# First loads of step B on other queues, with later stores and moved idle matmuls, in a fused FFT mixing and MoE kernel

## The chip, the cores and the metric

The kernel runs on one core of a Trainium2 chip. The metric is the device time of one execution in microseconds (us). Engines are named as in the profile: PE is TensorE (matmuls), PEld its weight loads, DVE is VectorE, ACT is ScalarE, POOL is GpSimd, SP is SyncE. SP, ACT and POOL each have a queue from which they issue DMA transfers; a transfer issued from such a queue waits in that engine's program order until what it reads is ready.

## The reference, cut to what matters

```python
X = np.fft.rfft(x, axis=1)                       # x: 4 x 3008 x 256
Xr, Xi = X.real, X.imag
Yr = Xr @ w_r - Xi @ w_i + b_r
Yi = Xr @ w_i + Xi @ w_r + b_i
Yr = sign(Yr) * maximum(abs(Yr) - 0.01, 0)
Yi = sign(Yi) * maximum(abs(Yi) - 0.01, 0)
y = np.fft.irfft(Yr + 1j * Yi, n=3008, axis=1)
x = y.reshape(12032, 256)
h = x @ w_in                                     # 256 x 2048, float64 weights
g = maximum(h, 0) + alpha * minimum(h, 0)
out = (g @ w_out).astype(float32)                # 2048 x 256
```

## The kernel before, in words

The sequence of 3008 is split as 47 x 64. For each of the four batches the transform and its inverse run in four steps, each a set of matmuls against a table.

Step A transforms along the 47 in 16 groups: `a_load` (L341) brings rows of x by SP, `a_mm` (L382) multiplies two matmuls a group into one of the three banks of `ps_f`, `a_evac` (L396) copies the bank to SBUF. For batch 0 the result stays in SBUF, in `a0_s`, and ScalarE and VectorE take turns at the copies. For the other batches ScalarE copies into a tile `ast`, and its store to DRAM is appended to a list, which `put` (L334) later issues from SP.

Step B transforms along the 64, in 12 pairs: `b_load` (L412) loads a pair in two halves of 128 KB into one of three buffers `bt`, for batch 0 out of `a0_s` by POOL, else by SP; `b_mm` (L423) multiplies with the table `rb_s`, `b_evac` (L432) takes the high part by ScalarE, `b_evac2` (L450) the low part by VectorE, and POOL then writes negated copies of a part of both (L457). The mix with w_r and w_i is `m_mm` (L465): a bias product (L471), then 24 matmuls (L478), in which the six with w_r come ahead of the six with w_i, twice; the ones with w_i read the negated copies. w_r and w_i are loaded raw (`load_mix`) and split into a high part by ScalarE and a low part by POOL (`split_mix`, L226). `m_evac` (L499) clips: ScalarE writes a tile `Yc` (L504), VectorE the output Y (L505). Step C (`c_mm`, `c_evac`, L545, L563) transforms back along the 64 and stores to DRAM from ScalarE's queue; step D transforms back along the 47 and feeds the two MoE layers, which fill the rest of the time from about 105 us on.

Beside all this the float64 weights of the MoE layers are converted into pairs of float32 parts. `conv_load` (L254) loads 512 KB of raw weights by SP into one of three slots; the conversion is a list of operations (`conv_first`, L265; `conv_second`, L280), of which `pump(n)` (L312) runs the next n, four for each raw weight once it is under way: the absolute value by ScalarE and a step of the weight before by VectorE (L275, L290), a clamp by VectorE (L276), two ScalarE, one VectorE and one POOL operation (L284 to L287), then VectorE and POOL operations (L293, L294, L277). A slot is free for the next load once L290 and L285 have read it.

The order of the work is written by hand. Batch 0's 16 groups of step A are followed by the first EARLY = 4 groups of batch 1 (L1006 to L1016). When the group n = NG is reached, batch 0's last group has just been evacuated. After that a loop over t (L1036) runs for each pair: the product of step B for pair t, the loads of pair t + 3, evacuations of the pairs before, the mix for pair t - 1, step C for pair t - 3, then PT[t] operations of the conversion, and some loads. `keep_warm(n)` (L985) issues n matmuls on a small tile of zeros that nobody reads. The last entry before the loop is `keep_warm(WARM)`.

The early groups' outputs use buffers that step B and C need later: the tags of `A1_TAGS` (L981) are, for the four groups, two of the buffers that step C copies into, then `Yt`, then `Yc`, which `m_evac` writes first for pair 0 in the loop's round 2.

Of the kernel before, what the change touches and what calls it, by code (L numbers as in the profile page):

```python
# [93 lines left out]
def fft_mix_moe(ctx, tc, x, w_r, w_i, b_r, b_i, w_in, w_out, alpha, la, rb, lc, rd, lf, cf, sel, out):  # L94
    nc = tc.nc
# [40 lines left out]
    def split(src, hi, lo, e_hi, e_lo):  # L136

        if e_hi is A:
            A.activation(out=hi, in_=src, func=AF.Copy)
        else:  # L140
            e_hi.tensor_copy(out=hi, in_=src)
        e_lo.tensor_tensor(out=lo, in0=src, in1=f(hi), op=ALU.subtract)
# [24 lines left out]
    def half(h):  # L167
        t = const.tile([128, 2, FH * 2 * C], F32R, tag=f"half{h}", name=f"w{h}")
        wi_h[h] = t[:, 0].rearrange("p (w k f) -> p w k f", w=2, k=CT)
        wo_h[h] = t[:, 1].rearrange("p (m w f) -> p m w f", w=2, f=C)  # L170

    def load_tables():
        nc.sync.dma_start(out=rd_s, in_=rd)
        nc.sync.dma_start(out=alpha_s, in_=alpha.rearrange("(k p) -> p k", p=128))
# [33 lines left out]
    def load_mix(*tags):  # L208
        for w, tag in zip((w_r, w_i), tags):
            t = work.tile([128, CT, C], F32, tag=tag, name="wm_f", bufs=1 if tag[1] in "tc" else None)  # L210
            nc.sync.dma_start(out=t, in_=w.rearrange("(k p) f -> p k f", p=128))
            mix_w.append(t)

    def load_rb(n0, n1):
        nc.sync.dma_start(out=rb_s[:, n0:n1], in_=rb[:, n0:n1])

    def load_cf(n0, n1):
        nc.gpsimd.dma_start(out=cf_s[:, n0:n1], in_=cf[:, n0:n1])
# [7 lines left out]
    def split_mix():  # L226
        for t, w in zip(mix_w, mix):
            split(t, w[:, 0], w[:, 1], A, G)
        mix_w.clear()
# [24 lines left out]
    def conv_load():  # L254

        m, i = divmod(conv_m[0], 2)
        conv_m[0] += 1
        k = conv_m[0] % 3
        raw = cw_s[:, NSLOT + 8 * k:NSLOT + 8 * k + 8].rearrange("p (k n) f -> p k (n f)", k=2)
        raw = raw.rearrange("p k (n w) -> p k n w", w=2)  # L260
        src = w_out.bitcast(U32)[256 * m:256 * m + 256] if i else w_in.bitcast(U32)[:, 512 * m:512 * m + 512]
        nc.sync.dma_start(out=raw.rearrange("p k n w -> p k (n w)"), in_=src.rearrange("(k p) f -> p k f", p=128))
        conv_raw.append((raw, m, i))
# [70 lines left out]
    def put(*queues):  # L334
        for n, (o, i) in enumerate(stores):
            (queues or (nc.sync,))[n % max(len(queues), 1)].dma_start(out=o, in_=i)
        stores.clear()
# [44 lines left out]
    def a_mm(b, g):  # L382
        ps = ps_f.tile([NQ, 2, C], F32, tag="f", name="ps_a")
        pa[b, g] = ps
        if b < 2:
            ts = x_rows(b, g)
            n = 2 // len(ts)
            for i, t in enumerate(ts):
                PE.matmul(ps[:, n * i:n * i + n], lf_s, t, start=True, stop=True)
            return  # L390
        hi, lo = xp.pop((b, g))
        PE.matmul(ps, la_s[:, 0], hi, start=True, stop=False)
        PE.matmul(ps, la_s[:, 1], hi, start=False, stop=False)
        PE.matmul(ps, la_s[:, 0], lo, start=False, stop=True)

    def a_evac(b, g):  # L396
        ps = pa.pop((b, g))
        if b == 0:
            st = a0_s[:, g]
        else:  # L400
            tag = A1_TAGS[g] if b == 1 and g < len(A1_TAGS) else "zst"
            st = work.tile([NQ, 2, C], F32, tag=tag, name="ast", bufs={"bt": 3, "zst": 3, "Yt": 1, "Yc": 1}.get(tag))
        if b == 0 and g % 2:
            V.tensor_copy(out=st, in_=ps)
        else:
            A.activation(out=st, in_=ps, func=AF.Copy)
        if b:
            stores.append((ad[b][:, 2 * g:2 * g + 2], st))

    bt, xs, xe, yc, ys = {}, {}, {}, {}, {}  # L410

    def b_load(b, q):  # L412
        t = work.tile([128, 2, C], F32, tag="bt", name="bt", bufs=3)
        if b == 0:
            src = a0_s.rearrange("(w s q) g r c -> q w s (g r) c", w=4, s=2)[q]
        else:
            src = ad[b].rearrange("(w s q) r c -> q w s r c", w=4, s=2)[q]

        for k in range(2):
            (nc.gpsimd if b == 0 else nc.sync).dma_start(out=t[:, k], in_=src[:, k])  # L420
        bt[b, q] = t

    def b_mm(b, q):  # L423
# [551 lines left out]
    EARLY = 4  # L975
    FILL = 14
    C0 = 2
    PT = [1, 2, 3, 3, 3, 3, 3, 3, 3, 3, 4, 4]
    TAIL = [['me', 1], ['ce', 3], ['cm', 2], ['cm', 1], ['ce', 2], ['ce', 1], ['d'], ['f', 4], ['e'], ['f', 6]]
    WARM = 70  # L980
    A1_TAGS = ("zst", "zst", "Yt", "Yc", "bt", "bt", "bt", "Xh", "Xl", "Xh", "Xl", "zst", "zst", "Yc")  # L981
    X1_TAGS = {4: ("Yl", "Yl"), 5: ("os", "Yt"), 6: ("gh",) * 4}
    idle = const.tile([128, 128], BF16, name="idle")
# [1 line left out]
    def keep_warm(n):  # L985
        ps = ps_f.tile([128, 512], F32, tag="f", name="ps_idle")
        for _ in range(n):
            PE.matmul(ps[:, 0:128], idle, idle, start=True, stop=True)

    with tc.manual_schedule():  # L990
# [8 lines left out]
        for g in range(EARLY // 2):  # L999
            a_load(1, g)  # L1000
        load_mix("Yh", "Yh")
        load_rb(4, 12)
        conv_tags.update(v1=("yh", "yl"), ex=("xh", "xh"), lf=("xl", "xl"))
        for _ in range(C0):
            conv_load()
        seq = [(0, g) for g in range(NG)] + [(1, g) for g in range(EARLY)]  # L1006

        for n, (b, g) in enumerate(seq):
            a_mm(b, g)
            if n >= 1:  # L1010
                a_evac(*seq[n - 1])
            if n == NG:
                for q in range(3):
                    b_load(0, q)
                split_mix()
                bias_parts()  # L1016
        a_evac(*seq[-1])
        half(0)
        put()
        load_tables()  # L1020
        keep_warm(WARM)

        def run(fn, q, *args):
            if 0 <= q < NPAIR:
                fn(0, q, *args)
# [8 lines left out]
                a1[0] = g + 1  # L1034

        for t in range(NPAIR + 1):  # L1036
            run(b_mm, t)
            run(b_load, t + 3)
            run(c_evac, t - 4)
            run(b_evac, t)  # L1040
            run(m_evac, t - 2)
            run(m_mm, t - 1, ps_h)
            run(b_evac2, t)
            run(c_mm, t - 3)
            if t < NPAIR:
                pump(PT[min(t, len(PT) - 1)])
            if t in (2, 5):
                load_rb(2 * t + 8, 2 * t + 14)
            if t < 8 and t % 2 == 0:
                load_cf(3 * t, 3 * t + 6)  # L1050
            if 5 <= t < 10:
                a_load(1, t - 3)
            if t == 10:
                half(1)
                conv_m[1] = FT
# [144 lines left out]
        for k in range(len(spairs) + SLAG):  # L1200
# [9 lines left out]
            if k >= SLAG:  # L1210
                n, t = spairs[k - SLAG]
# [43 lines left out]
```

## Time and profile before

| what | value |
|---|---|
| median of 3 runs | 1350.1 us (1348.96 to 1350.62) |
| the profiled execution's own time | 1350.56 us |
| its span in the profile | 1348.8 us |
| PE busy | 1335.5 us, 99% of the span |
| DVE, ACT, POOL busy | 77%, 56%, 28% |
| chain that ended last | PE 89%, DVE 3%, DMA 3% |

A row of a timeline gives the start and the duration in us, the engine, the source line, the operation, out<-in, the count, and in brackets how long the engine was idle before it and what ended that. Rows of SPq are DMA issues on SP's queue. A matmul's end is modelled, so rows of PE overlap by a little. Landing is the time from a DMA's issue to the semaphore that says that it is complete.

### The profile page before, as it was taken

What the parts mean: (1) busy time and instruction counts of PE and PEld (TensorE: products, weight loads), DVE (VectorE), ACT (ScalarE), POOL (GpSimd) and SP (SyncE); (2) the same over time, 40 slices, a digit from 0 to 9 for tenths busy, and PEclk for the clock granted to TensorE, in tenths of its full rate; (3) what the DMA queues carried; (4) which work ended last, traced back from release to release, by engine and by line L of the source; (5) the groups of instructions that cost most, each with busy time, mean ns of one, the idle gap of its engine ahead of it and who ended that gap; (6) DMA issues with size and microseconds to landing.
All of it is one profiled execution on the core that took longest, in us unless ns stands there. A gap on an engine that the chain in (4) does not pass through costs nothing.

```text
span 1348.8 us, 25138 instructions
## 1 busy us (share of the span) xinstructions
PE 1335.5 (99%) x9200; PEld 1250.7 (93%) x9200; DVE 1034.9 (77%) x1938; ACT 761.0 (56%) x1526; POOL 375.5 (28%) x400
## 2 busy tenths in 40 slices
PE   8999999999999999999999999999999999999998
PEld 4979999999999999999999999999999999999998
DVE  2767856776777777776768888888888888888885
ACT  3566655665566645555555555655555555555653
POOL 3864642222321222222221211121112111211222
PEclk9999999999999999999999999999999999999999
DMA  9974223342333312111110110111011101110001
GB/s 236 251 202 140 81 94 106 105 138 74 98 115 112 111 54 79 53 51 47 36 36 2 40 28 4 37 28 28 6 35 28 28 6 35 29 28 8 22 17 29
DMA packets 88119, 89.67 MB, mean 66 GB/s; under 512 B 42317, under 2 KB 70448, under 8 KB 87995
## 3 DMA queue, kind: packets, MB, share of 16 engines
q1 hardware_dynamic: 79700, 77.02, 20.1%
q0 software_dynamic: 5168, 8.02, 2.2%
q10 hardware_dynamic: 3127, 3.01, 0.7%
q8 instruction: 73, 1.20, 0.4%
q14 instruction: 51, 0.42, 0.1%
HBM read 50.49 MB, written 34.34 MB: 63 GB/s over the span
## 4 chain that ended last, share of the span: by engine, by line
PE 89%; DVE 3%; DMA 3%; issue 2%; ACT 1%; SPq 1%; POOL 0%; ACTq 0%; DVEq 0%; POOLq 0%
PE ps_h L794 24%; PE ps_h L689 13%; PE ps_m L491 6%; PE ps_o L895 6%; PE ps_o L896 6%; PE ps_o L894 6%; PE ps_d L620 4%; PE ps_o L728 3%; PE ps_o L727 3%; PE ps_o L726 3%; PE ps_b L428 2%; PE o_last L727 1%; PE o_last L728 1%; PE o_last L726 1%; PE o_last L894 1%
## 5 line engine op out<-in xcount | busy, mean ns | idle before, releaser
L794 PE MATMUL ps_h<-yh,w 128*128 128x512 f32 (+1 forms) x960 | 315.6, 389 | 0.0
L833 POOL TENSOR_TENSOR l<-t,h 128x512 fp32r<-128x512 f32 x98 | 127.0, 1296 | 496.5 <-ACT h L831 456.9
L794 PEld LDWEIGHTS ps_h<-yh,w 128*128 128x128 f32 x960 | 180.0, 188 | 33.2
L798 DVE SCALAR_TENSOR_TENSOR sq<-sq,beta_s,ps_h 128x512 f32<-128x512 f32 (+1 forms) x240 | 167.9, 732 | 54.5 <-ACT sq L797 53.6
L689 PE MATMUL ps_h<-yh,w 128*128 128x384 f32 (+1 forms) x704 | 207.0, 337 | 1.3 <-DVE q L696 1.3
L794 PE MATMUL ps_h<-yl,w 128*128 128x512 f32 (+1 forms) x480 | 186.2, 388 | 0.0
L696 DVE SCALAR_TENSOR_TENSOR q<-q,beta_s,ps_h 128x384 f32<-128x384 f32 (+1 forms) x192 | 115.1, 600 | 91.8 <-ACT q L695 90.9
L700 ACT ACTIVATE gh<-q 128x384 fp32r<-128x384 f32 (+1 forms) x192 | 99.1, 516 | 148.0 <-DVE q L696 145.3
L701 POOL TENSOR_TENSOR gl<-q,gh 128x384 fp32r<-128x384 f32 (+1 forms) x90 | 96.8, 1075 | 274.9 <-ACT gh L700 265.4
L813 ACT ACTIVATE dh<-sq 128x768 fp32r<-128x768 f32 x112 | 94.8, 846 | 117.8 <-DVE sq L798 75.8
L797 ACT ACTIVATE sq<-ps_h 128x512 f32<-128x512 f32 (+1 forms) x240 | 133.2, 586 | 26.9 <-PE ps_h L794 25.6
L689 PEld LDWEIGHTS ps_h<-yh,w 128*128 128x128 f32 x704 | 129.3, 189 | 4.4 <-DVE q L696 1.3
L695 ACT ACTIVATE q<-ps_h 128x384 f32<-128x384 f32 (+1 forms) x192 | 91.9, 479 | 62.1 <-PE ps_h L689 61.4
L831 ACT ACTIVATE h<-t 128x512 fp32r<-128x512 f32 x98 | 62.0, 633 | 105.2 <-DVE t L829 103.0
L689 PE MATMUL ps_h<-yl,w 128*128 128x384 f32 (+1 forms) x352 | 116.5, 331 | 0.0
L728 PE MATMUL ps_o<-w,gl 128*128 128x256 f32 x384 | 108.0, 281 | 0.6 <-POOL gl L701 0.6
L727 PE MATMUL ps_o<-w,gh 128*128 128x256 f32 x384 | 107.8, 281 | 0.0
L726 PE MATMUL ps_o<-w,gh 128*128 128x256 f32 x384 | 107.7, 280 | 0.0
L794 PEld LDWEIGHTS ps_h<-yl,w 128*128 128x128 f32 x480 | 90.5, 189 | 13.6
L828 DVE TENSOR_TENSOR dl<-sq,dh 128x768 fp32r<-128x768 f32 x98 | 93.4, 953 | 3.9 <-ACT dh L813 3.9
L896 PE MATMUL ps_o<-l,sw_a 128*128 128x256 f32 x294 | 82.0, 279 | 0.0
L894 PE MATMUL ps_o<-h,sw_a 128*128 128x256 f32 x294 | 81.9, 279 | 0.0
(214 smaller groups left out, 3618.5 us busy)
## 6 DMA issues: line engine op xcount, KB each, us to landing
zt<-zd SPq DMA_DIRECT2D x32, 384.0 KB
zd<-zst SPq DMA_DIRECT2D x37, 256.0 KB
ad<-ast SPq DMA_DIRECT2D x48, 192.0 KB
bt<-ad SPq DMA_DIRECT2D x72, 128.0 KB
xt<-in_x SPq DMA_DIRECT2D x21, 320.0 KB
out<-oT SPq DMA_DIRECT2D x152, 32.0 KB
cw_s<-in_moe_w_in SPq DMA_DIRECT2D x8, 512.0 KB
cw_s<-in_moe_w_out SPq DMA_DIRECT2D x8, 512.0 KB
```

Source lines behind the costliest of these rows:

```text
L689: PE.matmul(ps, wi_h[m // FH][:, w, ct, 128 * (m % FH):128 * (m % FH) + 128], a[:, ct, 0:n], start=(k == 0), stop=(k == 3 * CT - 1))
L696: V.scalar_tensor_tensor(out=q, in0=q, scalar=beta_s[:, m:m + 1], in1=ps, op0=ALU.mult, op1=ALU.add)
L700: A.activation(out=hi, in_=q, func=AF.Copy)
L726: PE.matmul(a, hi[:, t], w[:, 0], start=(i, k) in first, stop=False)
L727: PE.matmul(a, hi[:, t], w[:, 1], start=False, stop=False)
L728: PE.matmul(a, lo[:, t], w[:, 0], start=False, stop=(i, k) in last)
L794: PE.matmul(ps, wi_h[m // FH][:, w, ct, 128 * (m % FH):128 * (m % FH) + 128], a[:, ct, 0:w1], start=(k == 0), stop=(k == 3 * CT - 1))
L797: A.activation(out=q[:, j], in_=ps, func=AF.Relu, scale=-1.0)
L798: V.scalar_tensor_tensor(out=q[:, j], in0=q[:, j], scalar=beta_s[:, m:m + 1], in1=ps, op0=ALU.mult, op1=ALU.add)
L833: G.tensor_tensor(out=l24, in0=t24, in1=f(h24), op=ALU.subtract)
L894: PE.matmul(o, wh, gh, start=first, stop=False)
L896: PE.matmul(o, wh, gl, start=False, stop=last)
```

## The change

The loads of pairs 0 and 1 of step B are issued half by SP and half by ScalarE, and come ahead of the table part `load_rb(4, 12)` and the two first raw weights in SP's program; pair 2 stays with POOL. The split of the mixing weights goes behind the last evacuation of step A. The early groups' four stores (`put`) go from ahead of the loop to its round 1, and the two small tables of `load_tables` (the table of step D and alpha) to its round 6. The 70 idle matmuls ahead of the loop become 16, and 12 are issued at the head of round 1. PT has one operation fewer in rounds 0 and 1 and one more in rounds 8 and 9; the sum stays at 35.

```diff
-    def b_load(b, q):
+    def b_load(b, q, queues=None):
+        queues = queues or ((nc.sync,) * 2 if b else (nc.gpsimd,) * 2)
...
-            (nc.gpsimd if b == 0 else nc.sync).dma_start(out=t[:, k], in_=src[:, k])
+            queues[k].dma_start(out=t[:, k], in_=src[:, k])
...
-    PT = [1, 2, 3, 3, 3, 3, 3, 3, 3, 3, 4, 4]
+    PT = [0, 1, 3, 3, 3, 3, 3, 3, 4, 4, 4, 4]
...
-    WARM = 70
+    WARM = 16
...
         load_mix("Yh", "Yh")
-        load_rb(4, 12)
         conv_tags.update(v1=("yh", "yl"), ex=("xh", "xh"), lf=("xl", "xl"))
-        for _ in range(C0):
-            conv_load()
...
             if n == NG:
-                for q in range(3):
-                    b_load(0, q)
-                split_mix()
+                both = nc.sync, nc.scalar
+                b_load(0, 0, both)
+                b_load(0, 1, both)
+                load_rb(4, 12)
+                b_load(0, 2)
+                for _ in range(C0):
+                    conv_load()
                 bias_parts()
         a_evac(*seq[-1])
+        split_mix()
         half(0)
-        put()
-        load_tables()
         keep_warm(WARM)
...
         for t in range(NPAIR + 1):
+            if t == 1:
+                keep_warm(12)
             run(b_mm, t)
...
+            if t == 1:
+                put()
+            if t == 6:
+                load_tables()
             if 5 <= t < 10:
                 a_load(1, t - 3)
```

## Rows read from the trace of the kernel before

**Rows 1.** The page's busy times: engine, busy us, share of the span, instructions.

```profile
PE 1335.5 (99%) x9200; PEld 1250.7 (93%) x9200; DVE 1034.9 (77%) x1938; ACT 761.0 (56%) x1526; POOL 375.5 (28%) x400
```

**Rows 2.** Timeline of PE, from the start to pair 4 of step B.

```profile
1.00 4.02 PE L988 MATMUL ps_idle<-idle 128*128 128x128 bf16 x36 [1.00 <-DVE idle L991]
...
20.69 2.79 PE L389 MATMUL ps_a<-xt,lf_s 94*96 94x512 f32 x6 [0.78 <-DVE lam_s L199]
...
25.52 4.07 PE L988 MATMUL ps_idle<-idle 128*128 128x128 bf16 x70
30.42 1.80 PE L428 MATMUL ps_b<-rb_s,bt 128*128 128x128 f32 x12 [0.83 <-issue]
33.10 0.71 PE L428 MATMUL ps_b<-rb_s,bt 128*128 128x128 f32 x4 [0.87 <-DMA bt<-a]
...
34.59 0.40 PE L478 MATMUL ps_m<-wi_s,Xh 128*128 128x256 f32 x2
...
36.72 1.05 PE L428 MATMUL ps_b<-rb_s,bt 128*128 128x128 f32 x8
...
40.67 1.05 PE L428 MATMUL ps_b<-rb_s,bt 128*128 128x128 f32 x8
...
45.50 1.05 PE L428 MATMUL ps_b<-rb_s,bt 128*128 128x128 f32 x8
```

**Rows 3.** Timeline of POOL, 17 to 34 us.

```profile
21.29 4.11 POOL L420 DMA_DIRECT2D bt<-a  x6 [16.19 <-DVE bias_h L201]
25.51 1.28 POOL L142 TENSOR_TENSOR wr_s<-wm_f,wr_s 128x512 fp32r<-128x512 f32 x1
...
31.85 1.37 POOL L420 DMA_DIRECT2D bt<-a  x2 [3.85 <-PE ps_b L428]
33.25 0.41 POOL L457 TENSOR_SCALAR Xh<-Xh 128x256 fp32r<-128x256 f32 x1
```

**Rows 4.** Landing of step B's loads by POOL: the first half, then all 24 halves.

```profile
L420 POOL DMA_DIRECT2D bt<-a x1: 735/735/735, 21.3 to 21.3; - x1
DMA to landing us min/median/max: 9.0/9.0/9.0
...
L420 POOL DMA_DIRECT2D bt<-a x24: 679/690/807, 21.3 to 68.5; - x24
...
DMA to landing us min/median/max: 4.2/7.8/9.9
```

**Rows 5.** Windows: stretch, length, then PE, PEld, DVE, ACT, POOL busy, clock, DMA share, GB/s.

```profile
24.50:30.40 5.90, 5.01 (x72) 4.25 (x73) 0.00 (x0) 1.59 (x4) 3.40 (x4) 1.00 1.08 244
...
70.00:75.00 5.00, 5.00 (x41) 4.85 (x40) 4.86 (x7) 2.64 (x6) 4.37 (x4) 1.00 1.07 265
```

**Rows 6.** Timeline of ScalarE, 17 to 125 us.

```profile
22.70 0.63 ACT L139 ACTIVATE wr_s<-wm_f 128x512 fp32r<-128x512 f32 x1 [3.02 <-DMA wm_f<-in_w_r]
...
23.95 1.54 ACT L406 ACTIVATE ast<-ps_a 96x512 f32<-96x512 f32 x3
...
80.49 0.63 ACT L284 ACTIVATE w<-conv 128x512 fp32r<-128x512 f32 x1 [1.43 <-DVE conv L290]
```

**Rows 7.** Timeline of SP's DMA issues, 17 to 140 us.

```profile
24.55 4.61 SPq L336 DMA_DIRECT2D ad<-ast  x4
...
30.37 1.55 SPq L174 DMA_DIRECT2D alpha_s<-in_moe_alpha  x1
31.96 2.55 SPq L262 DMA_DIRECT2D cw_s<-in_moe_w_in  x1
...
62.10 4.58 SPq L360 DMA_DIRECT2D xt<-in_x  x4
...
70.24 9.29 SPq L360 DMA_DIRECT2D xt<-in_x  x12
```

**Rows 8.** Timeline of VectorE, 24 to 105 us: the clipped outputs of pairs 8 and 9.

```profile
78.58 0.68 DVE L505 SCALAR_TENSOR_TENSOR Y<-ps_m,Yc 128x512 f32<-128x512 f32 x1
...
83.89 0.69 DVE L505 SCALAR_TENSOR_TENSOR Y<-ps_m,Yc 128x512 f32<-128x512 f32 x1
```

## The prediction

> **What bounds the kernel now.** I read the page first: PE is busy for 99% of the span [rows 1]. Nothing of the change touches the bulk of PE's work, so it can only win where PE still waits, or lose where it makes PE wait; what is won before the long steady stretch stays won to the end, because everything behind it follows PE. A measurement of this kernel tells about 0.2% from no change, which is 2.7 us.
>
> PE's timeline comes next [rows 2]. The transforms of step A end near 25.5, the 70 idle matmuls fill 25.52 to 29.59, and the first product of step B starts at 30.42. Its next part waits again, at 33.10, and names the transfer bt<-a. From there PE has no gap: the product with w_i of the first pair starts at 34.59, pair 2 of step B at 36.72, pair 3 at 40.67, pair 4 at 45.50 (pairs count from 0). The prize therefore lies between 25.5 and 34.6.
>
> Why it waits is read from POOL and from the landings. POOL issues the six half loads of the first three pairs from 21.29 on, 0.69 us each [rows 3]; the first lands 9.0 us after its issue [rows 4], at 30.3, just ahead of PE's 30.42. So PE waits for the landing and for nothing else. The engines that carry the transfers are full meanwhile: share 1.08 in 24.5 to 30.4 [rows 5]. By the order of the program, SP has queued a 512 KB piece of the table and two raw weights of 512 KB before these loads are issued.
>
> ScalarE shows the second holder: it starts to split the mixing weights at 22.70, after 3.02 us of waiting for them, and takes the first outputs of the early groups out of PSUM only at 23.95 [rows 6].
>
> **The early part, step by step.** The change issues the halves of pairs 0 and 1 from SP and ScalarE as soon as the last group of batch 0 is out of PSUM. This adds a wait to ScalarE, whose evacuations of the early groups now stand behind two issues. POOL reacted to that group at 21.29, so I take 21.3 for both queues, and POOL's 0.69 us an issue as the upper price: ScalarE is free by 22.7. Moving the split behind them lets the early groups run on: three groups of transforms took 2.79 us from 20.69 [rows 2], so the fourth, which no longer waits for its bank, ends near 24.4. Its evacuation (three took 1.54 us together; 0.6 for one alone, with its latency, is my estimate) ends at 25.0, the two splits of 0.63 us [rows 6] at 25.6 and 26.3.
>
> From here POOL sets the pace. Its two low parts take 1.28 us each (the row of the first, taken for both [rows 3]): 25.6 to 28.2. In program order the two issues of pair 3 follow, 1.37 us, to 29.55, then the negation of Xh, 0.41 us, to 29.95. The product with w_i needs that negated part; it starts near 30.0 instead of 34.59. That is **4.6 us** gained, if pairs 0 and 1 land in time. The first must be multiplied before POOL reloads its buffer at 28.2; the stretch from the second half of pair 1 to the w_i product took 34.59 - 33.10 = 1.49 us, so pair 1 is needed by about 28.0. All landings of such loads lie between 4.2 and 9.9 us [rows 4]: 25.5 to 31.2 here. I take the low end, up to 26.5, because only the mixing weights are still ahead in the queue (ScalarE had the first at 22.70), no longer 1.5 MB. The idle matmuls, 16 and then 12 at 58 ns (4.07 us for 70) [rows 2], take 0.9 and 0.7 us and fit into time in which PE would wait for loads or for POOL anyway; without that cover they would cost at most these 1.6 us. The second block also takes one of the three banks in turn, which the evacuations have freed by then.
>
> What is late next is pair 3. Its loads are now issued at 28.2 and 28.9. Pair 2 would start at 30.0 + 2.13 (36.72 - 34.59) = 32.1, pair 3 at 32.1 + 3.95 = 36.1, its second half near 36.5. With the median landing, 7.8 us, the second half lands at 36.7: a stall of 0.2. At 9.9 us it is 2.3, below 7.6 us nothing. I take **0.5 us** lost.
>
> The stores of the four early groups move behind the raw weights in SP's program. They took 4.61 us to issue, from 24.55 [rows 7], and in SP's queue the raw weights stood ahead of them before, too. ScalarE writes over the last of these buffers when it clips pair 0, near 33.4, and PE needs that two pairs later, at 36.9 less two passes of 0.7: a store that lands by 35.5 costs nothing. Ends: 0 and 1 us; I take 0, since the stores leave SP at about the same time as before. The table part and raw weights queue behind at most 768 KB of step B's loads, some 3.1 us at the 244 GB/s of 24.5 to 30.4 [rows 5]; pair 2 at 32.1 is the first to need that part, so I cost this at nothing, ends 0 and 1.
>
> **The late part.** The change also does two conversion operations fewer at pairs 0 and 1 and one more at each of pairs 8 and 9, which then have four, as pairs 10 and 11 have. With four, VectorE went from one clipped output at 78.58 to the next at 83.89 [rows 8], 5.31 us, where PE needs 45.50 - 40.67 = 4.83 for a pair. Each such pair makes VectorE 0.48 us later; before, only pair 10 did so visibly, now 8, 9 and 10. I take two more, **1.0 us**, as lost at the end of step C; ends 0 (PE lets VectorE fall a little behind) and 2.0 (pair 11 as well, and a wait of ScalarE on top).
>
> The two small tables move to pair 6. Before, the second held SP for 1.55 us and the raw weight behind it for 2.55 [rows 7], early, where nobody waited. At pair 6 they stand ahead of input rows and the next raw weight, in a stretch where the transfers fill their engines again (1.07 in 70 to 75 [rows 5]). ScalarE reads raw weights at the head of a group; it had 1.43 us to spare there (80.49 [rows 6]). I cost this at 0, with ends 0 and about 6 (second rival).
>
> **The sum.** -4.6 + 0.5 + 1.0 = -3.1 us. The profiled execution took 1350.56 (span 1348.8), which gives 1347.5; the median of the runs, 1350.1, is 0.46 lower, so I forecast **1347.0**, or 0.23% faster: close to the limit of what can be told.
>
> **The rivals.** *The halves land no sooner.* If two queues into full engines take the 9 us that POOL's first load took, pair 0 is there at 30.3 and pair 1, issued 0.7 later, at 31.0. Behind pair 0 (0.8 us) and the 12 idle matmuls, pair 1 starts at 31.8; the w_i product follows 1.9 us later (0.4 + 1.49), at 33.7, and POOL's reload and negation are ready by then. The gain is 0.9; with the late 1.0 the sum is +0.1: 1350.2, no change. For it speaks the share of 1.08, against it that the queue ahead is shorter by 1.5 MB. The Trainium skill (DMA: Bandwidth & Descriptors, Rules for kernel authors) says that spreading transfers over issuing queues brings no bandwidth, since all share the same 16 engines and interleave; by it alone this rival would hold, and the sum would be +0.1. The trace agrees on full engines; the order in the queue is what the rule leaves out.
>
> *Raw weights hold ScalarE (slower).* At pairs 9 and 10, ScalarE stands in order before its conversion until the raw weight has landed, and behind it wait the evacuations that free PE's banks. The small tables delay SP by about 1.55 + 2.55 - 0.8 = 3.3 us (0.4 an ordinary issue, an estimate), and the input rows of pair 7, now ahead of the raw weight, by 4.58 [rows 7]; the reader comes about 3 us later in its pair than before. 3.3 + 4.6 - 3.0 - 1.4 to spare = 3.5 us, and about 3 more for the next weight, behind four of the twelve loads that took 9.29: 6.5 lost, 6.5 - 3.1 = 3.4 us slower, 1353.5. It decides when a raw weight lands over 1.4 us after its reader is ready, and turns the sign beyond 4.5. Against it: from pair 9 on, fewer other loads compete.
>
> *The clock falls.* The first 36 idle matmuls took 4.02 us, 112 ns each, against 58 ns for the 70 [rows 2]: that is the pace of 1.2 against 2.4 GHz, though the clock row says 1.00. With 28 idle matmuls for 70, two products of step B and one of the mix (40.67 - 36.72 + 0.8 = 4.75 us) could run at half pace, 4.75 us more, of which some 1.6 lie in PE's wait for POOL: -3.1 + 3.1 = 0, 1350.1. Against it: PE has less idle time after the change than in 29.6 to 33.1, where it kept its pace. The Trainium skill (TensorE: Matmul & The Clock Gate, What's actually happening) says that an idle array's clock is halved; by it the sum would be 0, but only if PE idles longer than it did before.
>
> *Nothing is given back.* If PE absorbs VectorE's lag and pair 3 is in time, 4.6 stay: 1345.5. Early pairs, where VectorE idles, speak for it.
>
> **How the numbers follow.** Forecast 0.52 (0.42 of it beyond 2.7 us, 0.10 within); nothing given back 0.14, faster; halves no sooner 0.12, no change; raw weights 0.16 (0.10 slower, 0.06 within); clock 0.06, no change. So faster 0.56, same 0.34, slower 0.10. The forecast's own bounds run from 1345.3 to 1349.5; with the rivals, 1345.0 to 1351.0 leaves out under 2 in 10.
>
> **What would show it.** Right: step B's first product near 25.5 to 27, the w_i product of pair 0 near 30, with POOL's negation just before it; pair 3 near 36 to 37; then a shift of about 4 us up to pair 8, of about 3 at the transforms behind step C. Wrong: bt landing after 28; ScalarE waiting for raw weights at pairs 9 and 10; PE idle over 1 us there; or idle matmuls at twice 58 ns.

## The result, and the profile of the kernel after

The kernel after takes 1359.02 us (median of 6 runs, 1357.69 to 1359.79) against 1350.36 for the kernel before on the same chip (1348.96 to 1352.59): the ratio is 1.0062, with a 95% interval of 1.0049 to 1.0075. It is 8.7 us slower, where 3.1 us less was forecast, and lies above the upper end of the range. The profiled execution took 1357.69 us with a span of 1355.9, 7.1 us more than before.

The page first. PE's busy time grew by 2.0 us [rows 1], so most of the loss is waiting:

```profile
PE 1337.5 (99%) x9158; PEld 1251.6 (92%) x9158; DVE 1034.2 (76%) x1938; ACT 760.2 (56%) x1526; POOL 371.1 (27%) x396
```

PE's timeline, from the idle matmuls to pair 4, then the bias products in the rounds of pairs 10 and 11, and the first product of step D (start, duration, in brackets the idle time and what ended it):

```profile
23.72 1.06 PE L989 MATMUL ps_idle<-idle 128*128 128x128 bf16 x16
27.62 1.13 PE L429 MATMUL ps_b<-rb_s,bt 128*128 128x128 f32 x8 [2.84 <-DMA bt<-a]
...
33.14 1.19 PE L429 MATMUL ps_b<-rb_s,bt 128*128 128x128 f32 x4 [3.73 <-DMA bt<-a]
34.95 1.22 PE L429 MATMUL ps_b<-rb_s,bt 128*128 128x128 f32 x4 [0.61 <-DMA bt<-a]
...
37.67 0.63 PE L479 MATMUL ps_m<-wi_s,Xh 128*128 128x256 f32 x2
...
40.76 1.06 PE L429 MATMUL ps_b<-rb_s,bt 128*128 128x128 f32 x8
...
44.72 1.05 PE L429 MATMUL ps_b<-rb_s,bt 128*128 128x128 f32 x8
...
49.54 1.05 PE L429 MATMUL ps_b<-rb_s,bt 128*128 128x128 f32 x8
...
80.61 0.50 PE L472 MATMUL ps_m<-bias_p,ones 128*128 128x512 f32 x1 [0.18 <-DVE Y L506]
...
86.47 0.50 PE L472 MATMUL ps_m<-bias_p,ones 128*128 128x512 f32 x1 [0.47 <-DVE Y L506]
...
108.30 2.87 PE L621 MATMUL ps_d<-rd_s,zt 96*128 96x94 f32 x24
```

The first product of step D in the kernel before:

```profile
101.19 2.87 PE L620 MATMUL ps_d<-rd_s,zt 96*128 96x94 f32 x24
```

Against [rows 2], pair 0 begins 2.8 us earlier, but pair 1 waits until 33.14 and 34.95 for its two halves, so the first product with w_i starts at 37.67 and not at 30; pair 2 is 4.04 us late, pair 4 as much. At the end of the stage, step D begins at 108.30 for 101.19, 7.11 us late, as much as the span grew; the MoE layers behind it add nothing.

The chain that ended last names the half that did it: pair 1's second half, issued by ScalarE, is under way for 13.37 us. Pair 2's halves, issued by POOL at the same time, land in 9.0 and 9.7 us, sooner than pair 1's.

```profile
20.35 1.14 ACTq L421
21.49 0.05 issue
21.54 13.37 DMA bt<-a
34.91 0.04 issue
34.95 1.22 PE ps_b L429 x4
```

The windows show two more things (columns as in [rows 5]). Just after the halves are issued, in 22 to 23 us, the transfer engines are at a share of 0.33, where the stretch of before was at 1.08 [rows 5]; by 24 to 25, with the table slots issued behind the halves, it is 0.95 again. And once PE has idled from 29.4 to 33.1, its granted clock is 0.50, the 1.2 GHz level, until 39.6:

```profile
22.00:23.00 1.00, 0.80 (x3) 0.22 (x2) 0.00 (x0) 0.86 (x2) 0.35 (x1) 1.00 0.33 79
...
29.40:33.10 3.70, 0.02 (x1) 0.00 (x0) 0.69 (x1) 0.00 (x0) 2.36 (x5) 0.98 1.09 336
33.10:39.60 6.50, 5.84 (x25) 5.48 (x26) 0.69 (x1) 1.16 (x2) 2.15 (x4) 0.50 0.89 269
```

SP's queue [rows 7]: its two halves at 20.35, then the table slots at 21.90 and the stores, which take 9.15 us to issue for 4.61. ScalarE in the late part [rows 6]: its own store issue is held from 76.0 to 78.2, and the next raw weight is waited for.

```profile
20.35 1.51 SPq L421 DMA_DIRECT2D bt<-a  x2
21.90 1.01 SPq L215 DMA_DIRECT2D rb_s<-tab_rb  x1
...
26.12 9.15 SPq L336 DMA_DIRECT2D ad<-ast  x4
```

```profile
78.19 0.37 ACTq L575 DMA_DIRECT2D zd<-zst  x1
78.66 0.60 ACT L443 ACTIVATE Xh<-ps_b 128x512 fp32r<-128x512 f32 x1 [2.62 <-DMA xt<-in_x]
...
81.76 0.67 ACT L275 ACTIVATE conv<-cw_s 128x512 f32<-128x512 f32 x1 [1.92 <-DMA cw_s<-in_moe_w_in]
```

### The profile page after: what moved, and what is told of

It is laid out like the page before. It is cut to its first block, busy times and chain, and to the rows that moved or that the text cites. A ratio compares the mean times of both kernels' runs of the same rounds, so it can differ in the third digit from the quotient of the medians.

```text
span 1355.9 us, 25054 instructions
## 1 busy us (share of the span) xinstructions
PE 1337.5 (99%) x9158; PEld 1251.6 (92%) x9158; DVE 1034.2 (76%) x1938; ACT 760.2 (56%) x1526; POOL 371.1 (27%) x396
## 4 chain that ended last, share of the span: by engine, by line
PE 93%; DMA 2%; DVE 2%; issue 1%; ACT 1%; POOL 0%; SPq 0%; ACTq 0%; DVEq 0%; POOLq 0%
PE ps_h L795 24%; PE ps_h L690 13%; PE ps_m L492 6%; PE ps_o L896 6%; PE ps_o L897 6%; PE ps_o L895 6%; PE ps_d L621 4%; PE ps_o L729 3%; PE ps_o L728 3%; PE ps_o L727 3%; PE ps_b L429 3%; PE ps_a L389 2%; PE ps_m L479 2%; PE o_last L728 1%; PE o_last L729 1%; PE o_last L727 1%
## 5 line engine op out<-in xcount | busy, mean ns | idle before, releaser
L795 PEld LDWEIGHTS ps_h<-yh,w 128*128 128x128 f32 x960 | 180.1, 188 | 33.1
```

The costliest lines, as they stand in the source:

```text
L795: PE.matmul(ps, wi_h[m // FH][:, w, ct, 128 * (m % FH):128 * (m % FH) + 128], a[:, ct, 0:w1], start=(k == 0), stop=(k == 3 * CT - 1))
```

## The experiments

Starts in us from PE's timeline: the first product of pairs 0, 2 and 9, and the first of step D. Times are medians, or one run where marked (1). The starts are those of one traced run, which can lie some us from the median: e9's took 1353.87, e10's 1362.54.

| kernel | pair 0 | pair 2 | pair 9 | step D | time, us | before beside it |
|---|---|---|---|---|---|---|
| before | 30.42 | 36.72 | 69.87 | 101.19 | 1350.36 | |
| after | 27.62 | 40.76 | 73.71 | 108.30 | 1359.02 | 1350.36 |
| e18_hold_hw | 27.51 | 40.92 | 73.96 | 110.26 | 1359.28 (1) | 1349.26 (1) |
| e7_hold | 26.35 | 33.49 | 75.82 | 110.32 | 1359.60 (1) | 1351.37 |
| e5_two_rows | 30.92 | 43.63 | 77.60 | 113.30 | 1362.97 (1) | 1350.60 |
| e1_pool | 29.13 | 36.43 | 70.09 | 104.05 | 1354.95 | 1350.60 |
| e4_idle | 27.83 | 39.37 | 72.32 | 106.56 | 1355.74 (1) | 1350.60 |
| e15_early_only | 27.40 | 42.29 | 77.10 | 110.02 | 1359.29 | 1350.39 |
| e2_old_pt | 27.78 | 40.01 | 73.15 | 109.67 | 1359.13 (1) | 1350.60 |
| e3_tables | 27.79 | 41.72 | 75.54 | 111.55 | 1360.67 (1) | 1351.37 |
| e6_all | 30.28 | 38.09 | 71.20 | 103.61 | 1352.91 | 1351.37 |
| e8_best | 25.98 | 33.14 | 78.11 | 109.81 | 1358.79 | 1351.37 |
| e9_put_first | 27.42 | 36.91 | 70.16 | 104.52 | 1356.66 | 1350.21 |
| e10_one_ahead | 29.57 | 35.40 | 71.88 | 112.59 | 1359.12 | 1350.21 |
| e11_four_ops | 30.54 | 36.19 | 69.32 | 107.11 | 1356.40 (1) | 1350.21 |
| e12_late_tables | 29.81 | 36.13 | 70.04 | 104.90 | 1354.26 (1) | 1350.21 |
| e13_tables10 | 29.20 | 35.37 | 68.53 | 103.06 | 1351.21 | 1350.39 |
| e14_held_put | 30.08 | 37.42 | 71.65 | 103.45 | 1353.15 | 1350.39 |
| e16_tables12 | 31.05 | 37.66 | 70.83 | 102.39 | 1351.33 | 1351.43 |
| e17_rb_split | 28.54 | 34.23 | 68.22 | 101.10 | 1350.52 | 1351.43 |

### Which queue carries the first pairs

**e7_hold and e18_hold_hw** are a pair: nothing but the mixing weights is ahead of pairs 0 and 1, and table slots and raw weights stay behind them. e7 is the kernel after with

```diff
-                both = nc.sync, nc.scalar
+                both = nc.gpsimd, nc.gpsimd
...
-                load_rb(4, 12)
                 b_load(0, 2)
-                for _ in range(C0):
-                    conv_load()
                 bias_parts()
         a_evac(*seq[-1])
+        last = dram.tile([1, 8], F32, tag="last", name="last", bufs=1)
+        nc.sync.dma_start(out=last, in_=stores[-1][1][0:1, 0, 0:8])
+        load_rb(4, 12)
+        for _ in range(C0):
+            conv_load()
```

and WARM = 30; e18 is the same without the first line, so SP and ScalarE load.

> The kernel after with pairs 0, 1 and 2 loaded by POOL and SP held until step A's last evacuation by a store of 32 bytes of that evacuation's tile, so that the convolution's table slots 4 to 11 and the raw weights are issued behind POOL's loads of pairs 0 and 1; 30 idle matmuls for 16 ahead of the loop, against a falling clock. Theory of order: only the mixing weights are then ahead of pairs 0 and 1, and they land 4 to 5 us behind their issue, by 26.5, as the prediction had it for the other queues; pair 0 by 26.6, pair 1 by 28.5, pair 2 by 34, and the time, with the late loss of 3 us still in it, about 1350 to 1351. Rival: what delays POOL's loads is not what is ahead of them but the total of transfers in flight, or POOL's own issuing; then they land 7 to 9 us behind their issue again and pair 2 begins at 36 to 37: 1354 to 1355.

> The run with SP held and POOL loading pairs 0, 1 and 2 (first product at 26.35, pair 1 at 29.05, landings 3.4 to 7.0 us), with the one difference that pairs 0 and 1 are loaded by SP and ScalarE, a half each, as in the kernel after; table slots and raw weights stay behind them. Theory: a half that reads 4 partitions is carried by only a few of the 16 transfer engines from these two queues, so it lands late with nothing else in flight too: transfer share under 0.5 in 22 to 25 us, first product at 27 or later, second half of pair 1 not before 30. Rival: the halves landed late in the kernel after because of the table slots and raw weights right behind them; then they land as POOL's do, first product by 26.5 and pair 1 by 29.1.

PE's timeline of e7_hold, then that of e18_hold_hw:

```profile
26.35 1.11 PE L429 MATMUL ps_b<-rb_s,bt 128*128 128x128 f32 x8
...
29.05 1.53 PE L429 MATMUL ps_b<-rb_s,bt 128*128 128x128 f32 x8 [0.92 <-DMA bt<-a]
...
45.94 0.80 PE L472 MATMUL ps_m<-bias_p,ones 128*128 128x512 f32 x1 [6.93 <-DVE Y L506]
```

```profile
27.51 1.13 PE L429 MATMUL ps_b<-rb_s,bt 128*128 128x128 f32 x8 [1.06 <-DMA bt<-a]
...
33.68 1.19 PE L429 MATMUL ps_b<-rb_s,bt 128*128 128x128 f32 x4 [4.37 <-DMA bt<-a]
35.58 1.22 PE L429 MATMUL ps_b<-rb_s,bt 128*128 128x128 f32 x4 [0.71 <-DMA bt<-a]
```

By POOL, the six halves land in 3.4 to 7.0 us and pair 1 is there at 29.05; by SP and ScalarE its second half comes at 35.58, 13.1 us behind its issue in the chain. Only the queues differ. The windows of e18 show engines with little to do up to 27 us, and full ones from 28 on:

```profile
22.00:23.00 1.00, 1.00 (x3) 0.16 (x1) 0.39 (x1) 0.00 (x0) 1.00 (x2) 1.00 0.13 43
...
26.00:27.00 1.00, 0.45 (x9) 0.28 (x5) 0.00 (x0) 0.44 (x1) 0.99 (x1) 1.00 0.29 67
...
28.00:29.00 1.00, 1.00 (x16) 0.99 (x16) 0.00 (x0) 0.32 (x1) 0.56 (x2) 1.00 1.01 334
```

So the queues make the halves late, as the theory said (only the window 24 to 25, at 0.53, was above its 0.5). The quiet ends when the table slots and raw weights follow, which SP issues from 25.73 on; pair 1's halves land in the full stretch behind that. So the pair of runs shows that the queue makes them late, and not how much of the 13.1 us is the queue's own pace and how much is what came behind. But e7 was not faster than e18 in the end, against what was expected of it: ScalarE waits 9.14 us for the early groups' stores before it may clip pair 0's mix into the buffer `Yc` (the 6.93 at 45.94). In that kernel the stores stand behind the raw weights.

```profile
44.41 0.69 ACT L505 ACTIVATE Yc<-ps_m,lam_s 128x512 f32<-128x512 f32 x1 [9.14 <-DMA ad<-ast]
```

**e5_two_rows** cuts each half of the kernel after into two transfers of two source rows on the same queue: `queues[k].dma_start(out=t[64 * h:64 * h + 64, k], in_=src[2 * h:2 * h + 2, k])` for h in 0, 1.

> The changed kernel with each half of pairs 0 and 1 cut in two transfers of two rows each, on the same queue. Theory A: the number of engines follows the rows that a transfer reads, so two engines now carry what four did; pair 0 lands some 6 us later than 27.6 and pair 1 some 12 us later than 33 to 35, and the time grows by 10 us or more. Theory B, or a limit of the rows that are read: the same bytes come from the same rows, pair 1 lands within 2 us of 33 to 35, and the time stays within 2 us of 1358.

```profile
25.00:29.00 4.00, 1.99 (x18) 1.23 (x18) 0.00 (x0) 3.19 (x6) 0.56 (x1) 1.00 0.14 44
29.00:33.00 4.00, 2.08 (x17) 2.04 (x18) 0.04 (x1) 0.60 (x1) 2.33 (x3) 0.83 0.16 49
```

For eight us the share stays at 0.14 to 0.16, close to two engines of sixteen (0.125). Apart from pair 2's halves by POOL little else is in flight then, for SP issues the table slots only afterwards:

```profile
32.12 0.85 SPq L215 DMA_DIRECT2D rb_s<-tab_rb  x1
```

So traffic from behind does not make this pace. Pairs 0 and 2 came 3.3 and 2.9 us later than in the kernel after, less than expected; the direction and the share fit. That a half of 4 rows runs on four engines is worked out from this and from the shares above, not seen engine by engine. An estimate from these rows: at twice 44 to 49 GB/s the four halves, 512 KB, would move in 5.4 to 6.0 us, so the rest of the 13 us would be due to the slots and raw weights that fill the engines from behind; no run loads whole halves by SP and ScalarE with nothing behind them. The Trainium skill (DMA: Bandwidth & Descriptors, Why a DMA increments its semaphore by 16 and not by 1) says the same of the number of engines: it is the largest up to 16 that divides the outermost size of both sides, here 4 and 128, and a hardware queue always takes the lowest-numbered ones, by which all four halves would share the same four. The shares of SP's and ScalarE's loads fit that rule, though no trace here tells the engines apart; POOL's loads of the same shape were quicker.

**e1_pool** is the kernel after with pairs 0 and 1 by POOL, SP not held.

> The changed kernel with one part undone: pairs 0 and 1 are loaded by POOL again, at the new place in the order. Theory A (few engines): a half issued from SP or ScalarE reads four rows (partitions) of SBUF and is carried by a few of the 16 transfer engines only, so it takes 12 us and more; POOL's loads use all of them. Then pair 1 lands by about 29 to 30 instead of 33.1 and 34.9, the clock stays at 2.4 GHz, pair 2 of step B starts near 34 instead of 40.8, and the time falls by about 6 us to 1352 to 1353. Theory B (full engines): the loads are slow because the engines are full, whoever issues them. Then pair 1 lands near 33 to 35 as before and the time stays at 1357 to 1360.

Pair 1 no longer waits, and half of the 8.7 us is gone: 4.35 are left (ratio to before 1.0031, 1.0020 to 1.0043). That is 2 us more than expected: pair 0 waits 3.92 us, the clock falls here too, to 0.50 from 29 to 32 us, and pair 2 begins at 36.43 and not at 34. POOL's issues hold only POOL, so SP runs ahead and its table slots and raw weights are in front of the pairs again, as in the kernel before.

### The clock

**e4_idle** is the kernel after with `keep_warm(90)` for `keep_warm(12)` at the head of round 1.

> The changed kernel with 90 idle matmuls at the head of round 1 instead of 12, so that PE is busy until about 33.8. If the half clock is a cost of its own, the granted clock stays at 1.00 after 33, the mix of pair 0 runs at 0.12 us a matmul, and pair 2 of step B starts near 38.5 instead of 40.8: 2 to 2.5 us less, about 1356. If something else bounds that stretch (POOL's negation, the table), pair 2 starts at 40.5 or later.

```profile
33.00:36.00 3.00, 3.00 (x51) 3.00 (x49) 0.00 (x0) 0.00 (x0) 0.00 (x0) 1.00 0.83 221
36.00:40.00 4.00, 4.00 (x35) 3.96 (x35) 0.69 (x1) 1.16 (x2) 2.15 (x4) 1.00 0.85 275
```

With PE at work in the wait the clock stays at 1.00, the 2.4 GHz level. Pair 2 begins 1.4 us earlier, step D 1.7, and the run is 3.3 us below the kernel after's median, 2.0 below its profiled run. By this one run the lost idle matmuls cost about 2 us.

### The late parts, alone and together

**e11_four_ops** and **e12_late_tables** put one late part each into the kernel before: `PT = [1, 2, 3, 3, 3, 3, 3, 3, 4, 4, 4, 4]`, and `load_tables()` in round 6 for ahead of the loop.

> The kernel before with the number of vector operations per pair changed alone, 4 for 3 at pairs 8 and 9. The prediction's term: 0.48 us at each, so the transforms behind step C begin 1.0 us later and the time is 1351.3. Theory from the kernel after and the run with POOL's loads alone, where each pair with four operations took 5.3 to 5.9 us for 4.83: pairs 10 and 11 begin later by 0.8 us each and the last bias too, 2 to 2.6 us in all, 1352.5.

> The kernel before with the table part (rd and alpha) issued at pair 6 for ahead of the loop, and nothing else. The prediction's term: 0. Theory from the run with the old list of operations, where the table part at pair 6 stood ahead of the rows on SP's queue and ScalarE's store issue was held 6.5 us behind it: 3 us or more, a wait at pairs 8 to 10, 1353 or more. Rival: that wait came of the shift of the pairs in that run, and the table part costs less than 0.5 us by itself.

Four operations for three at two pairs cost 5.9 us at step D, six times the forecast and over twice what the run itself was expected to show. VectorE's timeline of e11_four_ops, then POOL's:

```profile
80.29 0.67 DVE L505 SCALAR_TENSOR_TENSOR Y<-ps_m,Yc 128x512 f32<-128x512 f32 x1
...
82.62 1.50 DVE L277 TENSOR_SCALAR conv<-conv 128x512 uint32<-128x512 uint32 x1
84.16 1.65 DVE L290 SCALAR_TENSOR_TENSOR conv<-cw_s,conv 128x512 uint32<-128x512 uint32 x1
...
89.15 0.69 DVE L505 SCALAR_TENSOR_TENSOR Y<-ps_m,Yc 128x512 f32<-128x512 f32 x1 [2.81 <-ACT Yc L504]
...
97.53 0.42 DVE L277 TENSOR_SCALAR conv<-conv 128x512 uint32<-128x512 uint32 x1
97.98 0.69 DVE L290 SCALAR_TENSOR_TENSOR conv<-cw_s,conv 128x512 uint32<-128x512 uint32 x1
```

```profile
82.13 1.71 POOL L287 TENSOR_TENSOR conv<-conv 128x512 f32<-128x512 f32 x1
83.92 1.34 POOL L294 TENSOR_TENSOR w<-conv 128x512 fp32r<-128x512 f32 x1
```

Two of VectorE's steps, L277 and L290, take 1.50 and 1.65 us while POOL's tensor operations run beside them, each ending just after POOL's (84.12 behind 83.84, 85.81 behind 85.26), and 0.42 and 0.69 when POOL is idle. The same happens in the kernel before with three operations (1.51 at 71.14, 1.66 at 72.69); with four it comes to both steps at three pairs in a row. The clipped outputs of three successive pairs come at 68.30, 74.30 and 80.29, 6.0 us apart, where the prediction had 5.31. Then the lag turns into a wait: ScalarE's next operation reads L290's result (it waits 4.79 us), and the clip of the next pair stands behind it in order. The clipped outputs are 8.86 us apart and PE waits 4.53 us at 89.90.

The table part at pair 6 costs 3.7 us at step D. ScalarE copies step C's output at 65.41 and cannot issue its store before 70.63:

```profile
65.41 0.60 ACT L570 ACTIVATE zst<-ps_c 128x512 f32<-128x512 f32 x1 [1.13 <-PE ps_c L553]
70.63 0.37 ACTq L574 DMA_DIRECT2D zd<-zst  x1
```

SP's two issues behind the table part took 6.98 us there. The profile names no data that the store waits for; why the issue is held isn't recorded. That full transfer engines (share 1.16 in 60 to 65) hold it is argued, not shown, and e17_rb_split below speaks against it as the whole reason.

**e2_old_pt**, **e3_tables** and **e15_early_only** undo the late parts in the kernel after: the list of operations, the table part, and both.

> The changed kernel with the numbers of conversion operations per pair as before (1, 2, then 3, 4 at the last two). If four operations at pairs 8 and 9 cost the late part, pairs 9 and 10 take 4.8 us again instead of 5.7 and 5.6, and what is lost between pair 9 and the transforms behind step C shrinks from 3.3 us to 1.5 or less: 1356 or so. If the late loads behind the small tables cost it, the loss stays near 3.3 us.

> The kernel after, with the two loads of the table part (rd and alpha) issued ahead of the loop again, behind the half's tile, and not at pair 6. Theory: behind pair 8 the kernel after loses a further 3.3 us (pair 9 begins 3.84 us late, the transforms behind step C 7.11 us late) mainly because alpha's 2048 packets of 4 bytes now stand on SP's queue ahead of the rows and raw weights that ScalarE's vector steps and evacuations wait for; then the loss from pair 9 to the transforms falls from 3.3 to 1.0 us or less, and the time to about 1357. Rival: the loss is the four vector operations per pair from pair 8 on; then it stays at 3.3 us and the time at 1359. The early part, pairs 0 to 3, should stand as in the kernel after in either case, within 1 us.

> The kernel after with the old list of vector operations and the table part ahead of the loop again: what is left is the first two pairs by SP and ScalarE, the order of SP's queue, the stores, splits and idle matmuls. By the early part of the kernel after alone (pair 9 begins 3.84 us late) the time is 1354.2; each of the two late parts by itself cost 4 us (table part at pair 6) and 6 us (four operations at pairs 8 and 9) when put into the kernel before, together 10, though the kernel after is only 8.7 slower in all. Theory: the early shift and the late parts overlap, so this run shows 1354 to 1355 and the late parts together have cost only 4 to 5 us in the kernel after. Rival: the late parts compensate each other fully and the early part is nearly the whole loss: 1357 or more.

The rival of the last one holds: without any late part the time is 1359.29, ratio 1.0066 (1.0051 to 1.0082), the whole loss. The parts that cost 5.9 and 3.7 us alone pay for themselves here. With the old list ScalarE stands 7.64 us at 37.72 for a raw weight that the change has put behind the pairs, and with the table part early the stores take 14.60 us to issue; pair 9 is then 7.2 us late for 3.84. e2 and e3, one part each, are no better, and what was expected of both failed: from pair 9 to step D they lose 5.2 and 4.7 us more than the kernel before, where the kernel after loses 3.3. **e6_all** has POOL's loads and neither late part:

> The kernel after with pairs 0 and 1 loaded by POOL, the old list of vector operations per pair, and the table part ahead of the loop: what is left of the change is the place of the early groups' stores, of the splits, of the raw weights in the program and the idle matmuls (16 and 12 for 70). Theory: the early part stands as in the run with POOL's loads alone (pair 2 at 36.4, pair 3 at 41.1), and the late loss is gone (under 0.5 us from pair 9 to the transforms), so 1351 to 1352.5. Rival: the stores behind pair 1 or the clock at half pace cost something of their own that shows late; then 1354 or more.

1352.91 against 1351.37, ratio 1.0012 (1.0003 to 1.0022): what is left is the fewer idle matmuls, with a clock of 0.50 from 28 to 34 us, and the places of stores, splits and raw weights. The starts were missed: pair 2 begins at 38.09 and not at 36.4, and 1.1 us go behind pair 9. Without the late parts, then, the loss is 8.9 us with pairs 0 and 1 by SP and ScalarE (e15) and 1.5 us with them by POOL. With POOL's loads the late parts do cost something, 2.8 us (the loss is 4.35 in e1 and 1.54 in e6).

### Does an early start pay at all?

**e8_best, e9_put_first, e10_one_ahead** look for a version that keeps early pairs. e8 is e7_hold with neither late part; e9 holds SP by the stores themselves (`put()` ahead of `load_rb(4, 12)` and the raw weights); e10 lets the slots and one raw weight go ahead again. Both have the table part early, no operation at pair 0 and one (e10: two) at pair 1, then the old list, and 30 and 50 idle matmuls.

> The same as the run before it (POOL loads pairs 0 to 2, SP held), with the old list of vector operations per pair and the table part ahead of the loop. Theory: pairs 0 to 3 as in that run, and no late loss: if the order pays, transforms behind step C 2 to 3 us ahead of the kernel before, and 1347 to 1348.5, faster than both; if it doesn't pay, 1351.

> Pairs 0, 1 and 2 loaded by POOL as in the two runs with SP held, but now SP is held by the early groups' stores themselves (each waits for its evacuation), and the table slots 4 to 11, the raw weights and the table part follow behind them; the old list of vector operations per pair, but with none at pair 0 and one at pair 1, for the raw weights come later. Theory: pairs 0, 1 and 2 begin near 26, 29 and 33.5 as in the held runs, and since the stores are no longer behind the raw weights the evacuation of pair 0's mix finds its buffer free: no wait of 7 us at pair 2's bias. Then pair 3 begins by 37.5, pair 9 by 67 (before: 69.87), and the time is 1347 to 1348. Rival: the transfer engines, at a share near 1 from 30 to 85 us, set the pace of that whole stretch, and what the early pairs gain is lost to a late raw weight; then a wait of 2 us or more stands at one of pairs 4 to 11 and the time is 1350 or more.

> As the run with the stores first, but table slots 4 to 11 and one of the two raw weights (0.5 MB each) are issued ahead of POOL's loads, as in the kernel before, and 50 idle matmuls. Theory of order: with 1 MB of the 1.5 MB ahead again, pairs 0 and 1 land 2 to 3 us later than with nothing ahead: pair 0 at 28 to 28.5, pair 2 at 35.5, and the time 1348.5 to 1350, between the kernel before and the run with the stores first. Rival: what is ahead doesn't matter, only the sum of what is in flight; then pairs 0 to 2 stand as in that run.

All three lost. In e8 and e10 pair 2 begins 3.6 and 1.3 us before the kernel before's; then PE waits 6.83 us in e8 as it did in e7, and ScalarE 5.17 us in e10, at 47.93, for a raw weight. In e9 pairs 0 and 1 begin early, but the clock is at 0.53 in 30 to 35 us, pair 2 is no earlier than before, and 3.0 us more go behind pair 9.

**e13_tables10** and **e16_tables12** move only the table part of the kernel before, to rounds 10 and 12; **e14_held_put** adds to e13 a small store of pair 0's buffer ahead of the stores, to hold SP; **e17_rb_split** adds to e16

```diff
-        load_rb(4, 12)
+        load_rb(4, 6)
...
         put()
+        load_rb(6, 12)
```

> The kernel before with the table part (rd and alpha) issued at pair 10, behind the last rows that SP loads in this stage, for ahead of the loop; nothing else. Theory: the table part ahead of the loop takes transfer time from pairs 0 and 1 (with it early, pair 0 began at 30.3, without it at 29.1 in the two runs with POOL's loads and the new places), and at pair 6 it holds ScalarE's store issue; at pair 10 the transfer engines are half idle, so it costs nothing there. Pairs 0 to 2 begin 1 us earlier, nothing is lost late, 1349 to 1349.5. Rival: the earlier pairs change which vector operation meets which pair and late raw weight, and the gain is lost again: 1350 to 1352. Slower than 1353 if ScalarE's store issue is held at pairs 10 and 11 as it was at pair 7 or 8.

> The run before it, with SP held until the second half of pair 0 has landed (a store of 32 bytes of it) ahead of the early groups' stores. Theory: the stores (0.77 MB) no longer share the transfer engines with pairs 0 and 1, which then land 1 to 2 us earlier still: pair 0 at 27.5 to 28.5, pair 2 at 34.5 to 35.5; the stores land by 37, before pair 0's mix needs their buffer at 38; 1347.5 to 1349. Rival: the third raw weight, which now comes 4 us later on SP's queue, or the stores' buffer is waited for at pair 2 or 3, and the time is 1351 or more.

> The kernel before with the table part issued at the loop's last round, behind the stage's last raw weights on SP's queue, for ahead of the loop. With it at pair 10, pairs 0 to 9 began 1.3 us earlier, and all of that and 0.6 us more was lost when ScalarE waited 2.4 us at 85 us for a raw weight that now stood behind the table part. Theory: behind the raw weights it costs nothing, the 1.3 us stay, and the time is 1349 (1348.5 to 1349.5). Rival: the end of the stage is set by the raw weights' and rows' transfers, which begin no earlier; then the gain is lost at pairs 10 and 11 again and the time is that of the kernel before, 1350 to 1351.

> The run before it, with table slots 6 to 11 (0.38 MB) issued behind the early groups' stores and only slots 4 and 5 ahead of POOL's loads of pairs 0 to 2. Theory of order: 0.38 MB less of 1.5 MB ahead lets pairs 0 and 1 land a further 1 us earlier (0.38 MB at the 390 GB/s of that stretch), pair 3 finds its slots by 37, and the time is 1348 to 1348.5. Rival: the first pairs gain and the raw weights behind the slots come later, which is found at pairs 10 and 11: 1349 to 1350.5.

e17 shows best where an early start goes. Pairs 0 to 2 begin 1.9 to 2.5 us earlier and pairs 9 to 11 still 1.65, and step D begins at 101.10 for 101.19. The ratio is 0.9998 (0.9989 to 1.0007). Its ScalarE, then that of the kernel before, at the same place:

```profile
73.48 0.58 ACT L570 ACTIVATE zst<-ps_c 128x512 f32<-128x512 f32 x1
76.79 0.37 ACTq L574 DMA_DIRECT2D zd<-zst  x1
77.26 0.60 ACT L442 ACTIVATE Xh<-ps_b 128x512 fp32r<-128x512 f32 x1 [3.20 <-DMA xt<-in_x]
```

```profile
75.50 0.57 ACT L570 ACTIVATE zst<-ps_c 128x512 f32<-128x512 f32 x1
76.85 0.37 ACTq L574 DMA_DIRECT2D zd<-zst  x1
77.32 0.60 ACT L442 ACTIVATE Xh<-ps_b 128x512 fp32r<-128x512 f32 x1 [1.25 <-DMA xt<-in_x]
```

The copy is 2.0 us earlier, the store's issue at the same 76.8: the profile names the loads of input rows, which SP issues until 79.2 in e17 and 79.5 in the kernel before. By these rows the end of this stage is tied to those loads, not to when its pairs began; no run moves them, so this is read and not tested. The issue stays held although the share falls to 0.62 in 75 to 76 and 0.18 in 76 to 77, so full engines are not the whole reason. The rival was right about the time. The expected reason, order ahead of the first pairs, isn't shown: they came 0.7 to 1.1 us earlier than in e13, less than the 1.85 us by which two traces of the same early part differ (e13 and e16, below). In e13 a raw weight behind the table part took the gain (2.36 us at 85.48). In e14 the hold let go only at 31.39 and the first pairs gained next to nothing. e16's profiled run had pair 0 at 31.05, unlike e13's 29.20, with nothing changed between the two before pair 10; why is open, and it means that a start near pair 0 can differ by 1.85 us from one trace to the next. None of the kernels is faster than the kernel before.

## Why the prediction was wrong

- **What bounds the early part**: right. PE waits for the landing of bt, after as before. The path summed through ScalarE and POOL came out too: the negation of Xh began at 30.44 for 29.55.
- **The landing of pairs 0 and 1** is the step that failed: "I take the low end, up to 26.5, because only the mixing weights are still ahead". It took POOL's landings for a price of any queue. With only the mixing weights ahead, POOL's halves did land in 3.4 to 7.0 us (e7_hold), as the step argued; from SP and ScalarE the last took 13.1 to 13.4 us, on few engines and with table slots and raw weights close behind. The term of -4.6 measured +4.0 at pair 2. The first rival had the direction with no sooner than POOL; that it could be worse than POOL was in no rival.
- **The clock** fell, as the third rival said, for 6.5 us. Its argument against, that PE has less idle time, hung on the landing. It was priced at 3.1 us and e4_idle gives about 2.
- **"What is won before the long steady stretch stays won"** failed as well, and would have put a gain in doubt even with the halves in time: e17_rb_split wins 1.65 to 2.5 us up to pair 11 and ends where the kernel before ends.
- **Four operations** at pairs 8 and 9: forecast 1.0, ends 0 and 2; 5.9 alone. The 5.31 us came from one pair; in e11 two intervals in a row took 6.0, and then ScalarE's order made the next 8.86.
- **The table part** at pair 6: forecast 0, ends 0 and 6; 3.7 alone. The second rival had the place, ScalarE held among full transfers, though what was held first was its own store issue, and the raw weight only by 1.92 us. The 1.43 us "to spare" were misread: that row (80.49) is L284, which waits for VectorE's L290, and not the first reader of a raw weight, L275.
- **In the kernel after neither late part is a net cost**: without both it takes the same 1359.3. With the raw weights moved behind the pairs they were needed where they are. Costs of parts measured alone do not add here: 5.9 + 3.7 and the early part's 8.9 are more than twice the loss. Nor was the late loss a sum: with POOL's loads the two parts cost 2.8.
- **Stores**: 0 was right in the kernel after, where pair 0 is late. With early pairs they are worth 7 us (e7_hold): the bound of 1 us was too low.
- **The bounds**: the forecast's own, 1345.3 to 1349.5, don't follow from its terms. With nothing lost the sum is 1350.1 - 4.6 = 1345.5; with every end taken but the second rival's, -4.6 + 2.3 + 1 + 1 + 2, it is 1351.8.

## What to carry to other kernels

Before a load moves from one queue to another, ask how many transfer engines its shape gets there: with the same transfers ahead, halves out of 4 partitions landed in 3.4 to 7.0 us from POOL's queue and in up to 13.1 from SP's or ScalarE's, with the engines at most 0.6 busy in the first five us. An early start is only worth what the last wait of the same stage leaves of it: find that wait (here row loads and ScalarE's store issue at 76.8 us) before summing what the first pairs gain. And don't add up parts that share a queue: here two changes that cost 5.9 and 3.7 us alone cost nothing beside a third. A start read from one trace can be off by 1.85 us, so a shift of that size needs more than one trace.

## What was not expected of the hardware

- A half of 128 KB from 4 rows, issued by ScalarE, was under way for 13.1 us, although the share of the transfer engines was only 0.13 to 0.60 in its first five us (e18_hold_hw).
- VectorE's bit operation L277 took 1.50 us beside POOL's tensor operation, 0.42 without; L290 1.65 against 0.69 (e11_four_ops).
- ScalarE's own DMA issue was held 4.6 us (e12_late_tables, 66.0 to 70.63) and 2.7 us (e17_rb_split, 74.06 to 76.79) behind its finished copy, the second time with the transfer share down to 0.18 at its end.
